# The first MoE of a fused attention, MoE, MoE kernel in token groups of 256 and 512 instead of 256 and 320 by turns

## The chip, the cores and the metric

One Trainium2 chip (trn2); the kernel runs on one of its cores. The metric is the device time of one launch in microseconds (us), from the profile-independent timing of repeated runs; 917.83 us is the median of three runs of the kernel before (917.74 to 920.07).

## The reference

Inputs are q, k, v of 4 batches, 8 heads, 576 positions, head size 64, a row `s` per head, and the weights of two MoEs.

```python
scores = scale * np.matmul(q, k.transpose(0, 1, 3, 2))
cum = np.cumsum(np.maximum(s, 0.0), axis=-1)
bias = -(cum[:, :, :, None] - cum[:, :, None, :])
scores = np.where(causal, -1e9, scores + np.minimum(bias, 0.0))
attn = np.exp(scores - np.max(scores, axis=-1, keepdims=True))
attn = attn / (np.sum(attn, axis=-1, keepdims=True) + 1e-09)
x = attn @ v                          # as (2304 tokens, 512)
h = np.maximum(np.maximum(x @ w1, x @ w2), x @ w3)   # d_ff 768
x = h @ w_out                         # first MoE
return ((x @ w_a) * (x @ w_b)) @ w2_out              # second MoE, d_ff 1536
```

## The kernel before

Everything is fp32. The matmuls of the MoEs take two-term splits: an operand `x` is kept as `xh` (rounded to fp32r) and `xl = x - xh`, and a product is three matmuls, `wh*xh + wh*xl + wl*xh`.

**Attention.** Heads go in pairs (4 a batch), so there are 32 pairs, numbered 0 to 31. A batch's 576 queries are two steps: `R = 0` takes the first 256 queries (a short step), `R = 1` the other 320 (a long step, against all 576 keys). So there are 8 steps, 0 to 7, of 4 pairs each; even steps are short. In steps 0 to 2 the scores are plain fp32 matmuls (`f_unit0`, `f_unit`, `f_joint`); in steps 3 to 7 they are split ones (`s_unit0`, `s_unit`, `s_joint`), for which `split_qk` writes the next pair's q and k in split form into `KB1`, `KB2`, `QA1`, `QA2` (one buffer each). A pair goes through: scores on PE (tiles `f`, `s`, `fj`, `sj`), `softmax` (L398 row maximum on DVE, L405 exp on ACT, L409 and L410 on DVE, L415 scaling on POOL), transposes of the probabilities on PE (`ft`, `t`, `tj`) with ACT copies to `PF`, the product with v (`f_pv`, tile `fpv`), and `f_x`, which writes `Xh` (ACT) and `Xl` (DVE), the split input of the first MoE. V(i) below is the product with v of pair i, S(i) its scores, T(i) its transposes.

**First MoE.** `moe1_units` makes the 22 units of one group of tokens; a group is one step's 256 or 320 tokens. 18 gate units (`gate(m, g)`, tile `g`, L592) are 12 matmuls each, with 128x128 weights and the group's tokens as moving columns; ACT and DVE take the maximum of three (L598, L601) and split it into `hh`, `hl`. 4 output units (`outp(c)`, tile `o`, L620) are 18 matmuls each; their result `xo` is stored to `x2T` in DRAM. So a group is 216 + 72 = 288 matmuls whatever its width. The 24 weight tiles are loaded and split during steps 0 and 1 (`fetch_w1`, `conv_w`).

**Order.** All pieces are put on one axis, `stream`, whose position counts attention steps: the pieces of step n lie between n and n + 1, the MoE units of step n's tokens between n + 1.1 and n + 2.1 (the first group between 1.7 and 2.1). They are emitted in this order, the attention with a raised priority, and the framework's planner orders each engine's queue: by priority among what it reckons ready, so MoE matmuls fill the gaps that a pair's softmax leaves on PE. Each engine then runs its queue in order and waits on semaphores.

```python
m0 = stp + 1 + (M0 if stp == 0 else M1)
m1 = stp + 2 + M1
for n, (c, fn) in enumerate(units):
    todo.append((stp, n, fn))
    stream.append((m0 + (m1 - m0) * acc / tot + 1e-6, 0, m_next))
```

**Loads.** `load_pair` puts a pair's k, q and v into `kraw` and `qvraw`, two buffers each, on SP's queue; the loads of pair i + 2 are emitted behind V(i). `PF` has two buffers (`pt_tile`). `preset` fills the constant parts of `KB2`, `QA1`, `QA2` on POOL at the start.

**Behind the attention.** What is left of the first MoE at position 8 is run as the list `moe`; pieces that load and split the second MoE's first weights and inputs (`at(n)`: `more_raw`, `x2_load`, `x2_split`, `w2_pieces`) are put between its units. The second MoE (L1086) follows, by a seven-product scheme over 384 and then 256 columns.

Of the kernel before, what the change touches and what calls it, by code (L numbers as in the profile page):

```python
# [29 lines left out]
def kernel(  # L30
# [18 lines left out]
    nc = tc.nc  # L49
# [21 lines left out]
    QW = 2 * N1 + 64  # L71

# [22 lines left out]
    const = ctx.enter_context(tc.tile_pool(name="const", bufs=1, side="left"))  # L95
# [9 lines left out]
    wst = tc.alloc_tile_pool(name="wst", bufs=3, side="left")  # L105
    ap_ = tc.alloc_tile_pool(name="attn", bufs=1, side="right")


    ident = const.tile([P, P], F32, name="ident")
    make_identity(nc, ident)  # L110

    maskJ = const.tile([P, S // 2 + 4 * P], BF16, name="maskJ")
# [24 lines left out]
    def pt_tile(shape, dt, nm):  # L137
        return ap_.tile(shape, dt, tag="PT", bufs=2, name=nm)
# [17 lines left out]
    with tc.high_priority(5000):  # L156
        ones = pt_tile([SR, 2, 4 * N1], F32, "ones")[:, 0, : 2 * S]
        cs = pt_tile([SR, 2, 4 * N1], F32, "cs")
        sraw, cum = cs[:, 0, : 2 * S], cs[:, 1, : 2 * S]
# [16 lines left out]
    def store_tails():  # L176
        chl = [
            mp.tile([SR, KC * N1], F32R, tag=f"X{c}1", bufs=1, name=f"c{c}")
# [19 lines left out]
    KB1 = ap_.tile([P, 2, S], F32R, name="KB1")  # L198
    KB2 = ap_.tile([P, 2, S], F32R, name="KB2")
    QA1 = ap_.tile([P, QW], F32R, name="QA1")  # L200
    QA2 = ap_.tile([P, QW], F32R, name="QA2")
# [5 lines left out]
    def preset():  # L207
        nc.gpsimd.memset(f(QA1[:, N1 : N1 + 64]), 0.0)

# [43 lines left out]
    w1o = []  # L253
# [9 lines left out]
    NPRE = 4  # L263
    for p_, n0, n1 in zip(w1p, (0, 6, 11, 18), (6, 11, 18, NPRE - MF)):
        w1_tiles(p_, w1_keys[n0:n1])

    w1_raw = {}

    def fetch_w1(key):
        if key in w1_t:  # L270
            raw = wst.tile([P, WC, 2], I32, tag="wst", name="wraw")
        else:
            if key == w1_keys[NPRE - MF]:
                wst.release()
                w1o.append(
                    tc.alloc_tile_pool(name="w1o", bufs=1, side="left", reuse_waits="tile")
                )
            w1_tiles(w1o[0], [key])
            raw = w1o[0].tile([P, WC, 2], I32, tag="raw", bufs=1, name="wraw")
# [23 lines left out]
    rows_in = []  # L303

    def load_pair(b, p, R):
# [7 lines left out]
        WK, WQV = 2 * S, 2 * N1 + 5 * P  # L313
        if b == 0 and p >= 2 and R == 0 and plain:
            t = mp.tile([P, MF * N1], F32, tag="hh" if bp == 2 else "hl", bufs=1, name="kqv")
            kt_, qt_ = t[:, : 4 * Q0], t[:, 4 * Q0 :]
        else:
            kt_ = ap_.tile([P, WK], F32, tag="sk", bufs=2, name="kraw")
            qt_ = ap_.tile([P, WQV], F32, tag="sq", bufs=2, name="qvraw")
        kn = kt_[:, : 2 * nk]  # L320
        if plain and R == 0:
            qn, vn = kt_[:, 2 * nk : 4 * nk], qt_[:, : nb * P]
            nc.sync.dma_start(kt_[0:66, : 4 * nk], kq0[bp])
        else:
            qn, vn = qt_[:, : 2 * nq], qt_[:, 2 * nq : 2 * nq + nb * P]
        kn = kn.rearrange("p (h c) -> p h c", h=2)
        qn = qn.rearrange("p (h c) -> p h c", h=2)
        if plain:
# [17 lines left out]
        vn = vn.rearrange("p (b f) -> p b f", f=P)
# [7 lines left out]
    def k_tails(b, p, R):  # L354
        nk = Q0 if R == 0 else S
# [3 lines left out]
    def q_tails(b, p, R):  # L359
        nq = Q0 if R == 0 else N1  # L360
# [4 lines left out]
    def split_qk(b, p, R, kn, qn):  # L365
        nk = Q0 if R == 0 else S
# [53 lines left out]
    def smm(ps, p, h, q0, ksl):  # L420
        qs = slice(h * (N1 + 64) + q0, h * (N1 + 64) + q0 + P)
# [23 lines left out]
    def s_joint(p):  # L445

# [130 lines left out]
    def moe1_units(R, b, X):  # L577
        n = Q0 if R == 0 else N1
        col = b * S + (0 if R == 0 else Q0)
        st = {}  # L580

        def gate(m, g):
# [3 lines left out]
            Xh, Xl = X()  # L586
# [9 lines left out]
            if g == 0:  # L596
                st["h"] = mp.tile([P, N1], F32, tag="mt", bufs=2, name="hf")
# [5 lines left out]
            if g == 2:  # L603
                if m == 0:
                    st["hh"] = mp.tile([P, MF, N1], F32R, tag="hh", bufs=1, name="hh")
                    st["hl"] = mp.tile([P, MF, N1], F32R, tag="hl", bufs=1, name="hl")
# [3 lines left out]
        def outp(c):  # L610
# [13 lines left out]
            xo = mp.tile([P, N1], F32, tag="mt", bufs=2, name="xo")  # L624
# [16 lines left out]
    def fetch(i):  # L641
        if i < len(pairs) and i not in nat_of:
            b, R, p = pairs[i]
            nat_of[i] = load_pair(b, p, R)
# [19 lines left out]
    def do_split(i):  # L664
        if split_pair(i):
            b, R, p = pairs[i]
            q_tails(b, p, R)
# [4 lines left out]
    def attn_pieces(i, X):  # L672
# [867 lines left out]
```

## Time and profile before

| what | value |
| --- | --- |
| median of three runs | 917.83 us |
| the profiled execution's own time | 915.72 us |
| its span, first to last instruction | 913.9 us |
| PE busy | 900.2 us (98%), 6296 matmuls |
| DVE, ACT, POOL busy | 592.2, 378.9, 225.7 us |
| share of the chain that ended last: PE | 90% |
| of this, lines L592 and L620 (first MoE) | 25% and 9% |

The profile's busy time of a matmul runs from its start to the modelled end of its passage, and neighbours overlap: a group's mean (say 315 ns) is a duration and not what one more matmul costs. What it costs is its pitch, the distance of two starts. In the chain of work that ended last, stretches of one kind are merged with their time and count, and time by count is the pitch.

### The profile page before, as it was taken

To read this page: it belongs to the slowest core of one execution; us is meant where nothing else is said; L and a number is where in the kernel's file an instruction comes from. 1 tells how busy PE (TensorE), PEld (TensorE's weight loads), DVE (VectorE), ACT (ScalarE), POOL (GpSimd) and SP (SyncE) were. 2 spreads that over 40 slices of the span, in tenths; PEclk is the share of its full clock that TensorE was granted. 3 is DMA by queue.
4 is the path that set the end of the run, shared out by engine and by line. 5 is a ranking of instruction groups with operands and counts; after the bars stand their busy time and mean duration, and the time that the engine had idled before them with its cause. 6 is when DMAs were issued, how large, how long until landed. Compare 5 with 4: busy or idle time off the path is not lost.

```text
span 913.9 us, 17151 instructions
## 1 busy us (share of the span) xinstructions
PE 900.2 (98%) x6296; PEld 849.0 (93%) x6296; DVE 592.2 (65%) x1407; ACT 378.9 (41%) x879; POOL 225.7 (25%) x328
## 2 busy tenths in 40 slices
PE   7999999999999999999999999999999999999998
PEld 7677899989999989999899999999999998999998
DVE  4798535554465544555369567767675868996874
ACT  4665634555446564465433332322322222423321
POOL 6654302222123221232122102111111212321211
PEclk9999999999999999999999999999999999999999
DMA  5665332313223132221143214444443243254331
GB/s 169 224 202 175 90 87 73 98 42 101 70 85 97 43 91 80 85 85 54 41 149 134 88 53 155 152 150 145 144 159 107 107 146 122 77 165 158 117 116 47
DMA packets 55212, 102.36 MB, mean 112 GB/s; under 512 B 5736, under 2 KB 39432, under 8 KB 55128
## 3 DMA queue, kind: packets, MB, share of 16 engines
q1 hardware_dynamic: 50520, 96.54, 33.4%
q10 hardware_dynamic: 4608, 4.72, 1.6%
q8 instruction: 50, 0.82, 0.4%
q14 instruction: 34, 0.28, 0.1%
HBM read 77.29 MB, written 23.94 MB: 111 GB/s over the span
## 4 chain that ended last, share of the span: by engine, by line
PE 90%; DVE 4%; DMA 3%; issue 1%; SPq 1%; ACT 1%; POOL 0%; DVEq 0%; ACTq 0%; POOLq 0%
PE g L592 25%; PE X L1086 23%; PE Z L1086 11%; PE o L620 9%; PE Y L1086 6%; PE fpv L531 5%; PE t L545 3%; PE f L466 2%; PE s L422 2%; PE s L423 1%; DVE slot L897 1%; PE ft L508 1%; DMA wraw<-in_moe_w_dram 1%; PE tj L558 1%; PE sj L456 1%
## 5 line engine op out<-in xcount | busy, mean ns | idle before, releaser
L592 PE MATMUL g<-Xh,hg 128*128 128x256 f32 (+1 forms) x576 | 174.8, 305 | 0.5 <-ACT xo L625 0.5
L592 PE MATMUL g<-Xl,hg 128*128 128x256 f32 (+1 forms) x576 | 173.4, 301 | 0.0
L592 PE MATMUL g<-Xh,lg 128*128 128x256 f32 (+1 forms) x576 | 173.2, 301 | 0.0
L592 PEld LDWEIGHTS g<-Xh,hg 128*128 128x128 f32 x576 | 108.5, 189 | 4.4 <-issue 1.6
L592 PEld LDWEIGHTS g<-Xl,hg 128*128 128x128 f32 x576 | 108.9, 189 | 2.5 <-issue 1.4
L592 PEld LDWEIGHTS g<-Xh,lg 128*128 128x128 f32 x576 | 108.8, 189 | 1.2 <-issue 0.9
L1086 PE MATMUL X<-xh,wh 128*128 128x384 f32 x288 | 97.5, 339 | 1.5 <-ACT u L1127 0.6
L1086 PE MATMUL X<-xl,wh 128*128 128x384 f32 x288 | 96.9, 336 | 0.0
L1086 PE MATMUL X<-xh,wl 128*128 128x384 f32 x288 | 96.9, 337 | 0.0
L88 POOL TENSOR_SCALAR wh<-wval 128x256 fp32r<-128x256 f32 x84 | 41.5, 503 | 190.5 <-DVE wval L891 141.8
L1086 PE MATMUL X<-woh,slot 128*128 128x256 f32 x432 | 81.1, 281 | 0.5 <-ACT ob L1129 0.5
L415 POOL TENSOR_SCALAR P<-P,rs 128x128 f32<-128x128 f32 (+2 forms) x80 | 50.1, 631 | 91.4 <-DVE rs L410 75.0
L601 DVE TENSOR_TENSOR hf<-g,hf 128x256 f32<-128x256 f32 (+1 forms) x96 | 43.5, 453 | 41.5 <-PE g L592 39.4
L897 DVE TENSOR_TENSOR slot<-hraw,slot 128x768 fp32r<-128x768 f32 x60 | 60.5, 1031 | 14.9 <-POOL slot L88 13.7
L1086 PEld LDWEIGHTS X<-woh,slot 128*128 128x128 f32 x432 | 68.0, 189 | 0.7 <-ACT ob L1129 0.7
L897 DVE TENSOR_TENSOR u<-Z,u 128x384 f32<-128x384 f32 x72 | 39.6, 552 | 44.5 <-ACT u L1129 34.0
L405 ACT ACTIVATE P<-P,nm 128x128 f32<-128x128 f32 (+2 forms) x80 | 46.5, 582 | 32.7 <-DVE nm L398 27.1
L1086 PE MATMUL X<-wol,slot 128*128 128x256 f32 x216 | 60.1, 280 | 0.0
L620 PE MATMUL o<-hh,lo 128*128 128x256 f32 (+1 forms) x192 | 58.0, 306 | 0.0
L620 PE MATMUL o<-hl,ho 128*128 128x256 f32 (+1 forms) x192 | 57.8, 303 | 0.0
L620 PE MATMUL o<-hh,ho 128*128 128x256 f32 (+1 forms) x192 | 57.0, 302 | 0.3 <-ACT xo L625 0.3
L398 DVE CUSTOM_DVE_ANT_0 P<-s,maskJ 128x128 f32<-128x128 f32 (+2 forms) x80 | 40.5, 514 | 25.7 <-PE s L423 16.7
(165 smaller groups left out, 2255.9 us busy)
## 6 DMA issues: line engine op xcount, KB each, us to landing
hT<-u SPq DMA_DIRECT2D x72, 192.0 KB
hraw<-hT SPq DMA_DIRECT2D x36, 384.0 KB
wraw<-in_moe_w_dram SPq DMA_DIRECT2D x18, 512.0 KB
wraw<-in_moe_w_out_dram SPq DMA_DIRECT2D x18, 512.0 KB
qvraw<-in_qv_dram SPq DMA_DIRECT2D x12, 640.0 KB
kraw<-in_kT_dram SPq DMA_DIRECT2D x24, 288.0 KB
wraw<-in_moe_w_a_dram SPq DMA_DIRECT2D x12, 512.0 KB
wraw<-in_moe_w_b_dram SPq DMA_DIRECT2D x12, 512.0 KB
```

Source lines behind the costliest of these rows:

```text
L88: nc.gpsimd.tensor_scalar(o, i, scale, 1.0, op0=ALU.mult, op1=ALU.mult)
L398: nc.vector.tensor_tensor_reduce(pt[:, c0 : c0 + w], v_, m_, -scale, first, op0=ALU.add, op1=ALU.min, accum_out=nm[:, i : i + 1],)
L405: e_ = nc.scalar.activation(pt[:, c0:c1], pt[:, c0:c1], AF.Exp, bias=first, scale=-1.0, accum_out=sm[:, g : g + 1],)
L415: nc.gpsimd.tensor_scalar(pt[:, c0:c1], pt[:, c0:c1], rs[:, g : g + 1], 1.0, op0=ALU.mult, op1=ALU.mult,)
L422: nc.tensor.matmul(ps, QA1[:, qs], KB1[:, h, ksl], start=True, stop=False)
L531: nc.tensor.matmul(ps[h * D : h * D + D, c0:n], w, x, start=(t == 0), stop=(t == len(mm[h]) - 1),)
L545: nc.tensor.transpose(ps[:, j * P : j * P + P], pt[:, j * P : j * P + P], ident)
L592: nc.tensor.matmul(ps[:, :n], w[:, kk, :], x[:, kk, :], start=(i == 0), stop=(i == len(mm) - 1),)
L601: st["V"] = nc.vector.tensor_tensor(hf, ps[:, :n], hf, op=ALU.max)
L620: nc.tensor.matmul(ps[:, :n], w[:, c, :], x[:, m, :n], start=(i == 0), stop=(i == len(mm) - 1),)
L897: return {"V": nc.vector, "P": nc.gpsimd}[e].tensor_tensor(o, a, b, op=op)
L1086: nc.tensor.matmul(ps[:, :n], w, x, start=(first and i == 0), stop=(i == len(mm) - 1), skip_group_check=not first,)
```

## The change

The first MoE runs over groups of its own, `GR`: tokens 0 to 256, and then four times 512 (256 to 768, to 1280, to 1792, to 2304). `f_x` cuts a pair's columns where they cross a group's border. The gate and output units get positions of their own (`G0` to `G1` the gates, `G1` to `G2` the outputs). `X` of even groups lies in pool `xA`, of odd ones in `xB`, which earlier hold the weights' raw tiles and the cumulative sums' temporaries. To make room, `PF` of long steps and odd short pairs has one buffer and that of even short pairs another, smaller one; `kraw` and the q part have one buffer (plain even pairs have their own in a pool `px`), v has two; `KB1` to `QA2` take `px`'s place, so `preset` runs only when the first split pair comes (pair 12). The raw weight tile and the `xt` tile of the second MoE share one buffer, and the pieces between the last units lie at other units.

```diff
+    NG = 512
+    GR = [(0, Q0)] + [(c, c + NG) for c in range(Q0, NT, NG)]
...
-    def pt_tile(shape, dt, nm):
-        return ap_.tile(shape, dt, tag="PT", bufs=2, name=nm)
+    def pt_tile(R, p):
+        if R == 0 and p % 2 == 0:
+            return ap_.tile([P, 2, 3 * P], F32, tag="PT0", bufs=1, name="PF")
+        return ap_.tile([P, 2, 4 * N1], F32, tag="PT", bufs=1, name="PF")
...
     def preset():
+        px.release()
+        kqp.append(
+            tc.alloc_tile_pool(name="kb", bufs=1, side="right", reuse_waits="tile")
+        )
+        for nm, w in (("KB1", 2 * S), ("KB2", 2 * S), ("QA1", QW), ("QA2", QW)):
+            t = kqp[0].tile([P, w], F32R, name=nm)
...
+            if b == 1 and p == 3 and R == 0:
+                kt_ = px.tile([P, 4 * Q0], F32, name="kraw3")
+            else:
+                own = plain and p % 2 == 0
+                kt_ = (px if own else ap_).tile([P, 2 * S], F32, tag="sk", bufs=1, name="kraw")
+            vt_ = ap_.tile([P, 5 * P], F32, tag="sv", bufs=2, name="vraw")
...
-    def f_x(R, p, ps, Xh, Xl):
-        n = Q0 if R == 0 else N1
-        rnd("A", Xh[:, p, :], ps[:, :n])
-        sub("V", Xl[:, p, :], ps[:, :n], f(Xh[:, p, :]))
+    def f_x(b, R, p, ps):
+        c0 = b * S + (Q0 if R else 0)
+        c1 = c0 + (N1 if R else Q0)
+        for g, (g0, g1) in enumerate(GR):
+            a, e = max(c0, g0), min(c1, g1)
+            if a < e:
+                Xh, Xl = x_tiles(g)
+                o = slice(a - g0, e - g0)
+                v_ = ps[:, a - c0 : e - c0]
+                rnd("A", Xh[:, p, o], v_)
+                sub("V", Xl[:, p, o], v_, f(Xh[:, p, o]))
...
     def do_split(i):
         if split_pair(i):
             b, R, p = pairs[i]
+            if not kqp:
+                preset()
...
+    G0, G1, G2 = (1.7, 3.02, 5.02, 7.02, 8.0), (2.05, 3.95, 5.95, 7.95, 9.0), (3.0, 5.0, 7.0, 9.0, 9.9)
+    for grp in range(len(GR)):
+        units = moe1_units(grp)
+        k = 3 * MF
         for n, (c, fn) in enumerate(units):
-            todo.append((stp, n, fn))
-            stream.append((m0 + (m1 - m0) * acc / tot + 1e-6, 0, m_next))
-            acc += c
+            todo.append((grp, n, fn))
+            if n < k:
+                at_ = G0[grp] + (G1[grp] - G0[grp]) * n / k
+            else:
+                at_ = G1[grp] + (G2[grp] - G1[grp]) * (n - k) / (len(units) - k)
+            stream.append((at_ + 1e-6, 0, m_next))
...
     stream.append((0.1, 0, tails))
-    stream.append((0.5, 0, preset))
...
-    at(1)(lambda: x2_split(0, 0, 1, q0[0], EN, (0,)))
+    at(3)(lambda: x2_split(0, 0, 1, q0[0], EN, (0,)))
...
+    at(10)(lambda: x2_split(0, 1, 2, q0[0], EN, (0,)))
```

## Rows read from the trace of the kernel before

**Rows 1.** The page, 40 slices: PE's busy tenths and the granted TensorE clock.

```profile
PE   7999999999999999999999999999999999999998
...
PEclk9999999999999999999999999999999999999999
```

**Rows 2.** Chain that ended last, whole span: start, us, engine, tile, line, count.

```profile
194.70 4.07 PE g L592 x34
...
462.77 30.04 PE g L592 x203
```

**Rows 3.** The same chain from 225 to 275 us: a score of 512 columns.

```profile
269.73 0.23 PE s L422
```

**Rows 4.** PE and its weight loads by form: busy us, mean ns, idle before.

```profile
L592 PEld LDWEIGHTS g<-Xl,hg 128*128 128x128 f32 x576 | 108.9, 189 | 2.5 <-issue 1.4 <-DVE Xl L92 0.4
```

**Rows 5.** A stretch of step 2, L592 alone: PE busy (count), PEld busy (count), PEclk, DMA, GB/s.

```profile
113.00:150.00 37.00, 32.22 (x186) 28.13 (x187) 1.00 0.31 81
```

**Rows 6.** The stretch before it, L620 alone, same columns.

```profile
92.00:113.00 21.00, 10.71 (x69) 8.91 (x69) 1.00 0.31 91
```

**Rows 7.** PE in order of time, end of step 1 and step 2: start, us.

```profile
109.39 2.42 PE L531 MATMUL fpv<-PF,qvraw 128*64 128x320 f32 x20
111.74 0.87 PE L508 MATMUL ft<-ident,F 128*128 128x128 f32 x6
...
115.99 0.87 PE L531 MATMUL fpv<-PF,qvraw 128*64 128x256 f32 x8
...
120.00 0.38 PE L466 MATMUL f<-kraw 66*128 66x128 f32 x2
...
120.37 0.59 PE L466 MATMUL f<-kraw 66*128 66x256 f32 x2
...
121.26 0.87 PE L531 MATMUL fpv<-PF,qvraw 128*64 128x256 f32 x8
```

**Rows 8.** The same view, the last product with v of step 2.

```profile
148.74 0.87 PE L531 MATMUL fpv<-PF,qvraw 128*64 128x256 f32 x8
```

**Rows 9.** DVE, ACT and POOL by form from 100 to 450 us.

```profile
L398 DVE CUSTOM_DVE_ANT_0 P<-s,maskJ 128x256 f32<-128x256 f32 x16 | 6.6, 414 | 0.0
...
L398 DVE CUSTOM_DVE_ANT_0 P<-s,maskJ 128x128 f32<-128x128 f32 x16 | 4.6, 286 | 6.7 <-PE s L423 5.8 <-PE g L592 0.8
L405 ACT ACTIVATION_READ_ACCUMULATOR P<-P,nm 128x1 f32 x80 | 15.1, 189 | 0.0
...
L511 ACT COPY PF<-ft 128x384 f32<-128x384 f32 x24 | 11.1, 473 | 10.0 <-PE ft L508 9.7
...
L405 ACT ACTIVATE P<-P,nm 128x256 f32<-128x256 f32 x16 | 8.0, 501 | 0.7 <-DVE nm L398 0.7
...
L405 ACT ACTIVATE P<-P,nm 128x128 f32<-128x128 f32 x16 | 6.3, 397 | 1.7 <-DVE nm L398 0.8 <-DVE rs L410 0.6
L81 ACT ACTIVATE QA<-qvraw 128x512 fp32r<-128x512 f32 x8 | 5.0, 631 | 14.2 <-DMA qvraw<-in_qv_dram 14.2
...
L415 POOL TENSOR_SCALAR P<-P,rs 128x256 f32<-128x256 f32 x16 | 8.3, 516 | 0.0
```

**Rows 10.** All engines in order of time: a load's issue, and its reader.

```profile
222.03 5.30 SPq L343 DMA_DIRECT2D qvraw<-in_qv_dram  x2
...
225.17 0.63 ACT L81 ACTIVATE QA<-qvraw 128x512 fp32r<-128x512 f32 x1 [1.28 <-DMA qvraw<-in_qv_dram]
```

**Rows 11.** POOL in order of time: the longest fill of `preset`.

```profile
1.99 1.05 POOL L210 MEMSET KB<- 64x1152 f32 x1
```

**Rows 12.** PE in order of time: a product with v, the next pair's transposes.

```profile
203.83 2.42 PE L531 MATMUL fpv<-PF,qvraw 128*64 128x320 f32 x20
...
207.11 0.27 PE L558 MATMUL tj<-ident,PJ 128*128 128x128 f32 x1
```

**Rows 13.** Stretches near the start, columns PE, PEld, DVE, ACT, POOL, PEclk, DMA, GB/s.

```profile
12.00:14.00 2.00, 0.00 (x0) 0.00 (x0) 1.40 (x8) 1.75 (x7) 1.44 (x4) 1.00 0.14 37
...
16.00:20.00 4.00, 4.00 (x21) 3.86 (x20) 1.69 (x8) 0.70 (x1) 0.82 (x2) 0.57 0.94 309
```

More of the change, by code (lines that the diff above doesn't have):

```diff
@@ L71 @@
     QW = 2 * N1 + 64
+    NG = 512
+    GR = [(0, Q0)] + [(c, c + NG) for c in range(Q0, NT, NG)]
+    assert GR[-1][1] == NT and len(GR) == 5
     DLY0, DLY1, DLY2, DLY3 = 900, 400, 1500, 1000
@@ L195, in store_tails @@
             nc.sync.dma_start(dq[:, 1, 64:], b[:, 1, :256])
[L198 to L201, printed above, removed]
+    kqp = []
     def heads(t, r0, r1, n):
@@ L207, in preset @@
     def preset():
+        px.release()
[4 more added lines that the diff above has]
+            t = kqp[0].tile([P, w], F32R, name=nm)
+            kqp.append(t.rearrange("p (h c) -> p h c", h=2) if w == 2 * S else t)
+        _, KB1, KB2, QA1, QA2 = kqp
         nc.gpsimd.memset(f(QA1[:, N1 : N1 + 64]), 0.0)
@@ L261, in w1_tiles @@
             w1_t[key] = [pool.tile([P, WC], F32R, name=c + nm) for c in "hl"]
-    NPRE = 4
-    for p_, n0, n1 in zip(w1p, (0, 6, 11, 18), (6, 11, 18, NPRE - MF)):
+    for p_, n0, n1 in zip(w1p, (0, 6, 11, 18), (6, 11, 18, 24)):
         w1_tiles(p_, w1_keys[n0:n1])
     w1_raw = {}
+    wr2 = xA.tile([P, 2, 2 * WC], I32, tag="b", bufs=1, name="wraw")
+    wr1 = wst.tile([P, 2 * WC], I32, name="wraw")
+    wraws = [t.rearrange("p (c t) -> p c t", t=2) for t in (wr2[:, 0], wr2[:, 1], wr1)]
     def fetch_w1(key):
[L270 to L279, printed above, removed]
+        raw = wraws[w1_keys.index(key) % 3]
         if key[0] == "g":
@@ L354, in k_tails @@
     def k_tails(b, p, R):
+        _, KB1, KB2, QA1, QA2 = kqp
         nk = Q0 if R == 0 else S
@@ L359, in q_tails @@
     def q_tails(b, p, R):
+        _, KB1, KB2, QA1, QA2 = kqp
         nq = Q0 if R == 0 else N1
@@ L365, in split_qk @@
     def split_qk(b, p, R, kn, qn):
+        _, KB1, KB2, QA1, QA2 = kqp
         nk = Q0 if R == 0 else S
@@ L420, in smm @@
     def smm(ps, p, h, q0, ksl):
+        _, KB1, KB2, QA1, QA2 = kqp
         qs = slice(h * (N1 + 64) + q0, h * (N1 + 64) + q0 + P)
@@ L445, in s_joint @@
     def s_joint(p):
+        _, KB1, KB2, QA1, QA2 = kqp
         HS = S // 2
@@ L643, in fetch @@
             b, R, p = pairs[i]
-            nat_of[i] = load_pair(b, p, R)
+            if i < NP:
+                nat_of[i] = load_pair(b, p, R)
+            else:
+                with tc.issue_after(last_in[-1] if i > NP else rows_in[NP - 1]):
+                    nat_of[i] = load_pair(b, p, R)
     def split_pair(i):
@@ L764 @@
                 fetch(i)
-        fetch_w1(w1_keys[2])
+        with tc.issue_after(rows_in[2]):
+            fetch_w1(w1_keys[2])
     stream = []
@@ L770, with x_tiles @@
     xt = {}
-    def x_tiles(stp):
-        if stp not in xt:
-            while todo and todo[0][0] <= stp - 2 and todo[0][1] < 3 * MF:
+    def x_tiles(g):
+        if g not in xt:
+            while any(t[0] <= g - 2 and t[1] < 3 * MF for t in todo):
                 todo.pop(0)[2]()
-            R = stp % 2
-            n = N1 if R else Q0
-            xt[stp] = [
-                mp.tile([P, KC, n], F32R, tag=f"X{c}{R}", bufs=1, name=f"X{c}")
-                for c in "hl"
-            ]
-        return xt[stp]
+            n = GR[g][1] - GR[g][0]
+            if g == 0:
+                t = xA.tile([P, 2, KC, n], F32R, tag="a", bufs=1, name="X")
+                xt[g] = [t[:, 0], t[:, 1]]
+            elif g % 2 == 0:
+                if g == 2:
+                    while w1_pend:
+                        load_w1(w1_pend.pop(0))
+                    wst.release()
+                xt[g] = [
+                    xA.tile([P, KC, n], F32R, tag=t, bufs=1, name=f"X{c}")
+                    for t, c in zip("ab", "hl")
+                ]
+            else:
+                xt[g] = [
+                    xB.tile([P, KC, n], F32R, tag=f"X{c}", bufs=1, name=f"X{c}")
+                    for c in "hl"
+                ]
+        return xt[g]
     def m_next():
@@ L836 @@
             fn()
+    assert not any(t[0] < len(GR) - 1 and t[1] < 3 * MF for t in todo)
     moe = [(1, m_next) for _ in range(len(todo))]
+    kqp[0].release()
     ap_.release()
+    xB.release()
     TB = 384
@@ L870, in load_raw @@
         nraw[0] += 1
-        raw = pool.tile([P, WC, 2], I32, tag="raw", bufs=1, name="wraw")
+        if pool is rA2:
+            t = pool.tile([P, 4 * TB], I32, tag="xt", bufs=1, name="wraw")
+            raw = t[:, : 2 * WC].rearrange("p (c t) -> p c t", t=2)
+        else:
+            raw = pool.tile([P, WC, 2], I32, tag="raw", bufs=1, name="wraw")
         rv = raw.rearrange("p c t -> p (c t)")
```

101 lines of the change are left out of this document (49 added, 52 removed).

## The prediction

> **What bounds the kernel now.** I read the slices of the page first. PE is busy in nearly every slice and its granted clock is at the upper level, 2.4 GHz, almost throughout [rows 1]. The reader is to see that no stage behind the first 20 us has a hole that a faster DVE, ACT or DMA would close. The chain of waits says the same: 90% of it is PE, and 34% is the first MoE (table above). So what matters is how long PE takes for a matmul, and whether it always has one to do. For the first I use the chain in order of time, where a run of one kind gives the pitch. For the second I use the stretch tables and PE's order of time around steps 1 and 2, because there the attention has the least MoE work beside it.
>
> **Part 1, wider groups.** Each group costs 288 matmuls whatever its width. Before there are 8 groups, 1152 matmuls of 256 columns and 1152 of 320; after there are one of 256 and four of 512, so 288 and 1152. 864 matmuls go; the columns stay the same.
> Pitches: 34 gate matmuls of 256 columns in 4.07 us are 0.120 us each, 203 of 320 columns in 30.04 us are 0.148 us [rows 2]. At 2.4 GHz the columns alone are 0.107 and 0.133 us, so 13 to 15 ns are fixed in each. Before: 1152 x (0.120 + 0.148) = 308.7 us.
> There is no gate of 512 columns in the trace, but there are fp32r scores of 512. The one shown takes 0.23 us [rows 3]; over seven couples of such scores (48 in all), by the distance of their starts, I read 0.2315. The columns are 0.213 us, so the fixed part would be 18 ns. With the fixed part of the narrower gates it would be 0.228. I take 0.230, nearest to the measured row, and keep 0.228 and 0.2315 as the bounds.
> After: 288 x 0.120 + 1152 x 0.230 = 34.6 + 265.0 = 299.6 us. Gain 9.1 us (7.4 to 11.4). It lies on PE, hence on the path.
>
> **Part 2, where the MoE work lies: step 2.** A wide group can begin only when all its tokens are through the attention. Group 0 is unchanged and is done early: 69 of its 72 output matmuls run between 92 and 113 us [rows 6]. In the 37 us that follow, the next group supplies 186 gate matmuls [rows 5], 186 x 0.148 = 27.5 us, and leaves about 9.5 us to the attention of step 2, whose last product, V(11), comes at 148.7 [rows 8]. Afterwards nothing of this exists: the next group (256 to 768) needs all four pairs of step 2. PE then has only the attention of pairs 8 to 11 until V(11) and its split are done.
> How long is that? The chain of one plain pair, from its first score: 0.95 scores of one head [rows 7], and from [rows 9] 0.70 maxima, 2 x 1.28 for the exps of two heads (each 0.397 + 0.189 + 0.501 + 0.189), 2 x 0.516 scalings, 0.47 copy. With about 0.3 for the small DVE ones, 0.3 for three transposes and 0.87 for V [rows 7] that is 7.2 us. ACT alone needs 2 x 1.28 + 2 x 0.47 + some 0.4 = 3.9 us a pair, so that is the floor of the pace. T(8) is at 111.7 us and V(8) at 116.0 [rows 7], with gates between; without them V(8) follows its copies at about 113.3, and V(9) at 116. S(10) can start when T(8) gives its buffers free, 112.4, so V(10) ends near 119.6 and V(11), a floor later, near 123.5; with the split 124.3. Between 113.6 and 124.3 PE has 9.2 us of scores, transposes and products (3.4 us for each of two whole pairs, 2.4 us for what is left of two). Hole: 1.5 us.
> `preset` moves into this place. Its fills, some of them over 1 us [rows 11], are then on POOL behind S(11), ahead of or between the scalings of pair 11; V(11) waits for those, and pair 12's splits and small SP loads queue behind the fills. I price it at up to 2 us. Pair 12's own wait is hidden by 216 gates, 49.7 us; without these it would be about 4 us of fills and a load. I take 3 us for the hole (1 to 12). The upper end is pairs one by one, 7.2 us each from V(9) at 117 on, so V(11) at 131.4, 9.4 us of hole, and a fall of the clock. The latter exists here: after PE was empty from 12 to 14 us, the granted clock of 16 to 20 us was 0.57, mostly the lower level, 1.2 GHz [rows 13], worth some 1.7 us.
>
> **Part 3, steps 4 and 6.** Gates now lie in long steps, outputs in short ones. A short step has 72 x 0.230 = 16.6 us of outputs and about 2.5 us a pair of attention, 26.5 us, or 6.6 us a pair, where it had some 11. ACT's floor for a split pair is 3.9 + 2 x 0.63 = 5.2 us [rows 9]. One k and q buffer makes a loop: split of pair i + 1, then the load of i + 2, then its split. The split is about 2 us on ACT and DVE; a load was read 3.1 us after its issue [rows 10], so 5 to 6 us with the other issues on SP. Both floors lie just under 6.6. Beyond that PE waits. A pair fully in series, 7.2 + 2, would cost 4 x 2.6 = 10.4 us a step. I take 0.75 us a step, 1.5 in all (0 to 21). The long steps have 49.7 us of gates and are safe.
>
> **Part 4, what I cost at nothing.** One `PF`: already before, the next pair's first transposes in a long step come behind V, which ends at 206.2, at 207.1 [rows 12], so the copy into `PF` meets a free buffer; if it did not, each long pair would wait 2.4 us. Loads of i + 2: on SP their q and k now wait for the split of i + 1, which lies ahead of V(i), and only v waits for V(i), so they come no later; without that lead a load's 3.1 us would lie between pairs. The columns cut at a border add one more ACT and one more DVE instruction to 12 pairs, about 0.3 us each behind V, where PE has other work. The shared raw and `xt` buffer and the moved pieces lie beside 26 units, 4 x 18 x 0.230 + 66.2 = 82.8 us of pure PE work, where 52 us held them before. The second MoE is untouched.
>
> **Sum.** -9.1 + 3 + 1.5 = -4.6 us. Against the profiled execution's own 915.72 that is 911.1 (its span 913.9 to about 909.3); that execution is 2.1 us under the median of the runs, 917.83, and on the median's scale the forecast is 913.2.
>
> **Rivals.**
> *A, even.* The gain is paid back: pairs of steps 4 and 6 at 7.4 us instead of 6.6 cost 6.4 us, the hole 3. Time 918.1. For it: floors of 5 to 6 us stand so near 6.6. Against it: the planner has the attention lead the MoE, so at the end of a long step some gates are left over.
> *B, slower.* The same place, short steps 4 and 6, decides: with a pace of 8 us a pair they cost 4 x 1.4 x 2 = 11.2 us, step 2 stays at 3, together 14.2 against 9.1. Time 922.9. The point from which it decides is a pace of about 7.4 us, where loss and gain meet. For it speaks the full chain of 7.2 us, which overlaps only if scores of the next pair are ready early, and they need the single buffers of `QA1` and k; against it that scores do run ahead: S(10) starts at 120.0 us, V(9) at 121.3 [rows 7].
> *C, a better pitch.* A weight load takes 189 ns [rows 4], longer than a matmul of 256 or 320 columns and shorter than 512. If the fixed part is what is left of that load, it goes: 1152 x (0.230 - 0.213) = 19.6 us more, time 893.6. Against it stands 0.23 [rows 3], fixed part and all. The Trainium skill, "TensorE: Matmul & The Clock Gate", section "Wait — 56ns, not 53.3ns?", states a warm pitch of 215.7 ns at 512 columns, a fixed cost of about 2.5 ns. By it the gain would be 16.5 us larger. Trace and page differ on the narrower gates already, and the measured row decides.
> *D, it does not do what it says.* The gates of 512 columns run at 0.235 or more and the planner pulls them apart by attention pieces: 1152 x 0.235 + 34.6 = 305.3, a gain of 3.4 us, eaten by the hole. Time about 918.9.
>
> **Chances and range.** Forecast 0.50, A 0.20, B 0.20, C 0.04, D 0.06. The forecast's own range, with pitch, hole and short steps at their nearer bounds, is 906 to 916. 0.3% is 2.75 us, about what a measurement of this kernel can tell from no change, so the lines are 915.1 and 920.6. Faster: nearly all of the forecast and C, 0.51. Within: A, D and the forecast's upper tail, 0.28. Slower: B, 0.21. The range must hold 8 in 10: it leaves out C and half of B, 905 to 924.
>
> **What would show it.** Right: L592 and L620 rows of 512 columns, whose runs in the chain give 0.228 to 0.2315 us; PE with few matmuls for 10 us around 115 to 124 us, then gates without a break; steps 4 and 6 with an interval of 6 to 7 us between products with v; a second MoE of the same length. Wrong: a pitch of 0.235 or of 0.216; gaps of PE on `ft` or `s` in short steps that wait for POOL, ACT or a load; a clock under 1.00 in the slices of step 2; ACT copies to `PF` that wait for `fpv`.

## The result: slower by 0.8%

The changed kernel takes 926.67 us (median of four runs, 925.01 to 927.39), the kernel before beside it 918.69: ratio 1.0083, 95% interval 1.0062 to 1.0104. The forecast was 913.2 us, with a range of 905 to 924 us. The two profiled executions differ by more than the medians, 925.6 against 913.9 us of span, because that of before is one of its shortest and that of after its longest. A term of 1 or 2 us that rests on one trace is therefore within what two executions of one kernel can differ.

**The page of after**, its header, PE's busy time, and the slices that answer to [rows 1]:

```profile
span 925.6 us, 15336 instructions
...
PE 906.0 (98%) x5432; PEld 794.6 (86%) x5432; DVE 587.2 (63%) x1365; ACT 376.1 (41%) x843; POOL 222.3 (24%) x328
...
PE   7999979999999999999999999999999999999998
...
PEclk8999999999999999999999999999999999999999
```

864 matmuls are gone, as forecast, and PE is as busy as before. Only one slice behind the start has lost its 9: the sixth, 116 to 139 us, which is step 2.

**Wide gates in the chain of work that ended last** (start, us, line, count), in answer to [rows 2]:

```profile
446.48 48.51 PE g L615 x214
497.93 9.78 PE o L643 x42
```

48.51 / 214 is a pitch of 0.2267 us, a little below the lower bound of the forecast (0.228). The fixed part beyond 512 columns at 2.4 GHz is 0.0134 us, the same 13 to 15 ns that the narrow gates have. The outputs' run, 9.78 / 42, is at 0.233 us, a little over the upper bound (0.2315).

**Step 2 of after, stretches of 5 us**: PE, PEld, DVE, ACT and POOL busy (count), granted clock, DMA share, GB/s.

```profile
126.00:131.00 5.00, 4.53 (x24) 3.66 (x24) 2.64 (x17) 2.29 (x10) 1.65 (x4) 1.00 0.30 87
131.00:136.00 5.00, 0.94 (x8) 0.62 (x6) 2.31 (x9) 3.25 (x8) 4.33 (x7) 0.86 0.50 147
136.00:141.00 5.00, 4.90 (x19) 3.56 (x20) 2.56 (x5) 2.19 (x9) 3.23 (x5) 0.50 0.14 26
141.00:146.00 5.00, 5.00 (x29) 3.86 (x28) 2.15 (x9) 2.07 (x5) 0.75 (x1) 0.95 0.88 244
```

PE is empty for 4 us, and the clock then falls to its lower level, 1.2 GHz, for some 7 us (what 0.86, 0.50 and 0.95 lack in three stretches of 5 us). **PE in order of time there**, in answer to [rows 7, 8]; in brackets what it waited for:

```profile
116.06 2.42 PE L548 MATMUL fpv<-PF,vraw 128*64 128x320 f32 x20
...
121.12 0.87 PE L548 MATMUL fpv<-PF,vraw 128*64 128x256 f32 x8
...
124.82 0.87 PE L548 MATMUL fpv<-PF,vraw 128*64 128x256 f32 x8
125.62 1.58 PE L483 MATMUL f<-kraw 66*128 66x128 f32 x8
...
136.10 0.58 PE L473 MATMUL sj<-KB,QA 128*128 128x288 f32 x1 [4.16 <-ACT KB L84]
...
137.33 1.55 PE L548 MATMUL fpv<-PF,vraw 128*64 128x256 f32 x8
```

V(7) comes at 116.1 us, 6.7 later than before. S(10) starts at 125.6, where before it started at 120.0 [rows 7]. The joint scores of pair 12 (`sj`) stand in PE's queue ahead of V(10) and wait 4.16 us for a split. V(11) is at 143.5.

**The chain in that stretch** says what the split waited for:

```profile
118.53 0.34 SPq L350
...
118.96 3.29 DMA kraw<-in_kq_dram
...
122.28 0.55 SPq L348
...
122.88 0.54 SPq L349
...
123.52 0.35 SPq L350
...
123.91 3.37 DMA kraw<-in_kq_dram
...
129.99 3.69 DMA kraw<-in_kT_dram
...
134.84 1.17 ACT KB L84
...
136.10 0.58 PE sj L473
```

A loop of loads on SP: k and q of pair 10 behind a load of v (L350), k and q of pair 11 behind the next one, then pair 12's. The first of these loads, v of pair 9, waits for V(7), 116.1 to 118.5 us. The second, v of pair 10, waits for no product: V(8) ended at 122.0. It stands behind the row copies of pair 10 (L348, L349), which start at 122.28, when that pair's k and q have landed. So each further pair comes about 5 us behind the one before it. **SP's own order** shows how that differs from before. First before, then after (L323 and L333 are k and q, L338 and L350 v):

```profile
84.47 0.31 SPq L323 DMA_DIRECT2D kraw<-in_kq_dram  x1
...
99.90 0.32 SPq L323 DMA_DIRECT2D kraw<-in_kq_dram  x1
104.26 0.31 SPq L323 DMA_DIRECT2D kraw<-in_kq_dram  x1
109.15 0.36 SPq L323 DMA_DIRECT2D kraw<-in_kq_dram  x1
113.88 8.62 SPq L338 DMA_DIRECT2D qvraw<-in_qv_dram  x3
```

```profile
89.13 0.37 SPq L333 DMA_DIRECT2D kraw<-in_kq_dram  x1
105.53 0.34 SPq L350 DMA_DIRECT2D vraw<-in_qv_dram  x1
107.20 0.32 SPq L333 DMA_DIRECT2D kraw<-in_kq_dram  x1
118.53 0.34 SPq L350 DMA_DIRECT2D vraw<-in_qv_dram  x1
118.96 0.32 SPq L333 DMA_DIRECT2D kraw<-in_kq_dram  x1
123.52 0.35 SPq L350 DMA_DIRECT2D vraw<-in_qv_dram  x1
123.91 0.38 SPq L333 DMA_DIRECT2D kraw<-in_kq_dram  x1
```

Before, k and q of pairs 8 to 11 are all issued by 109.2 us and the v of the later ones after them. After, each load of k and q follows a load of v, and pair 11's is issued at 123.9. The lines that do this belong to the change, but the cut diff ahead does not print them:

```diff
     def fetch(i):
         if i < len(pairs) and i not in nat_of:
             b, R, p = pairs[i]
-            nat_of[i] = load_pair(b, p, R)
+            if i < NP:
+                nat_of[i] = load_pair(b, p, R)
+            else:
+                with tc.issue_after(last_in[-1] if i > NP else rows_in[NP - 1]):
+                    nat_of[i] = load_pair(b, p, R)
```

`last_in[-1]` is the v load of the pair before. In SP's queue, which runs in order, k and q of pair i + 1 so stand behind v of pair i, and that one waits until V(i - 2) has given back one of the two v buffers, as v of pair 9 does here.

### Where the time lies

For a ledger I take three instants, V(7), V(11) and the second MoE's first product. From each I subtract the first MoE's matmuls started by then, at their pitch in a run (0.120, 0.148, 0.2267 us). What is left is attention plus every loss, so narrow and wide groups can be compared. At V(11), for instance, before has 288 matmuls of 256 columns and 185 of 320, 61.9 of 148.7 us, and after 288 and 27 of 512, 40.7 of 143.5. The columns are what is left up to V(7), from there to V(11), and from there to the second MoE's start.

| kernel | to V(7) | to V(11) | to MoE 2 | MoE 2 starts | MoE 2 to its last product |
| --- | --- | --- | --- | --- | --- |
| before | 75.8 | 11.0 | 108.4 | 503.9 | 406.5 |
| after | 83.4 | 19.4 | 114.2 | 512.7 | 409.4 |
| loads free (e1) | 79.0 | 15.4 | 114.1 | 504.3 | 408.4 |
| loads free, `sj` late (e3) | 77.5 | 13.0 | 116.0 | 502.2 | 409.3 |
| old groups, after's loads (e4) | 84.2 | 11.5 | 108.5 | 512.9 | 431.9 |
| old groups, loads free (e6) | 77.9 | 11.5 | 109.4 | 507.7 | 429.4 |
| before, after's loads (e5) | 80.1 | 11.1 | 110.4 | 510.4 | 406.4 |
| before, one `PF` (e8) | 77.0 | 11.7 | 108.4 | 505.7 | 406.3 |
| before, mask moved (e9) | 75.5 | 11.0 | 108.4 | 503.7 | 408.5 |

From before to after: the first MoE's own work falls by 13 us, what is left grows by 7.6, 8.4 and 5.8, and the second MoE by 2.9. Together that is the 11.7 us between the two spans.

Part of the first column is not the kernel's. The granted clock from 10 to 25 us is 0.89 in the traces of before, e3, e5, e6 and e9 and 0.77 in those of after, e1, e4 and e8; 0.12 x 15 us is up to 1.8 us of PE's work, an estimate. So e1 and after can be compared there, and e5 and before, but e1 with before, or e8 with before, only to within that.

### The profile page after: what moved, and what is told of

It reads as the page before. It is cut to its first block, busy times and chain, and to the rows that moved or that the text cites. A ratio compares the mean times of both kernels' runs of the same rounds, so it can differ in the third digit from the quotient of the medians.

```text
span 925.6 us, 15336 instructions
## 1 busy us (share of the span) xinstructions
PE 906.0 (98%) x5432; PEld 794.6 (86%) x5432; DVE 587.2 (63%) x1365; ACT 376.1 (41%) x843; POOL 222.3 (24%) x328
## 4 chain that ended last, share of the span: by engine, by line
PE 90%; DMA 4%; DVE 3%; issue 1%; SPq 1%; ACT 1%; POOL 0%; DVEq 0%; ACTq 0%
PE g L615 24%; PE X L1142 22%; PE Z L1142 11%; PE o L643 8%; PE fpv L548 6%; PE Y L1142 6%; PE t L569 3%; PE f L483 2%; PE s L438 2%; PE s L439 1%; PE ft L525 1%; DMA kraw<-in_kq_dram 1%; DVE slot L946 1%; PE tj L582 1%; PE spin L160 1%
## 5 line engine op out<-in xcount | busy, mean ns | idle before, releaser
L615 PE MATMUL g<-Xl,hg 128*128 128x512 f32 x288 | 113.1, 394 | 0.0
L615 PE MATMUL g<-Xh,lg 128*128 128x512 f32 x288 | 111.9, 393 | 0.0
L615 PE MATMUL g<-Xh,hg 128*128 128x512 f32 x288 | 111.7, 398 | 0.0
L615 PEld LDWEIGHTS g<-Xh,lg 128*128 128x128 f32 x288 | 54.1, 188 | 10.2
L615 PEld LDWEIGHTS g<-Xh,hg 128*128 128x128 f32 x288 | 54.3, 190 | 9.9
L615 PEld LDWEIGHTS g<-Xl,hg 128*128 128x128 f32 x288 | 54.1, 188 | 10.0
L624 DVE TENSOR_TENSOR hf<-g,hf 128x512 f32<-128x512 f32 (+1 forms) x60 | 38.0, 634 | 37.9 <-PE g L615 32.8
L548 PE MATMUL fpv<-PF,vraw 128*64 128x320 f32 (+4 forms) x432 | 58.6, 373 | 0.0
L1142 PEld LDWEIGHTS X<-xh,wh 128*128 128x128 f32 x288 | 54.1, 188 | 3.4 <-ACT s L1179 1.1
L91 POOL TENSOR_SCALAR slot<-hraw 128x768 fp32r<-128x768 f32 x25 | 29.9, 1197 | 106.4 <-PE Z L1142 35.1
```

The costliest lines, as they stand in the source:

```text
L91: nc.gpsimd.tensor_scalar(o, i, scale, 1.0, op0=ALU.mult, op1=ALU.mult)
L548: nc.tensor.matmul(ps[h * D : h * D + D, c0:n], w, x, start=(t == 0), stop=(t == len(mm[h]) - 1),)
L615: nc.tensor.matmul(ps[:, :n], w[:, kk, :], x[:, kk, :], start=(i == 0), stop=(i == len(mm) - 1),)
L624: st["V"] = nc.vector.tensor_tensor(hf, ps[:, :n], hf, op=ALU.max)
L1142: nc.tensor.matmul(ps[:, :n], w, x, start=(first and i == 0), stop=(i == len(mm) - 1), skip_group_check=not first,)
```

## The experiments

Theory L: the order of the loads costs the time. Rival S: the scores of pair 12 that stand ahead of V(10) on PE do. Further rivals: the wide groups themselves, the smaller buffers, the place in memory.

### Loads free, scores late, both (e1, e2, e3)

e1 is after with `fetch` as before:

```diff
-            if i < NP:
-                nat_of[i] = load_pair(b, p, R)
-            else:
-                with tc.issue_after(last_in[-1] if i > NP else rows_in[NP - 1]):
-                    nat_of[i] = load_pair(b, p, R)
+            nat_of[i] = load_pair(b, p, R)
```

> The changed kernel (926.7 us) with one thing undone: a pair's loads are no longer ordered behind the load of v of the pair before on SP's queue. Theory L (late loads: in steps 1 and 2 k of the next pair stands on SP behind a load of v that waits for the product with v of two pairs earlier, so with no MoE work beside it the attention of step 2 runs at the pace of the loads): V(7) comes some us earlier than 116.1, V(11) comes at 130 to 135 instead of 143.5, time 916 to 920. Rival S (the scores of pair 12 stand on PE ahead of V(10) and wait for preset and splits): the wait of 4 to 5 us on PE stays, time 924 to 927. Rival F (nothing but the missing MoE work in step 2): V(11) at 140 or later, time 925 to 927.

Measured: 918.84 us, ratio to before 1.0001 (0.9981 to 1.0020). By the ratios, each within some 2 us, this one edit takes back the whole loss. By the medians, after is 7.98 us over the kernel before beside it and e1 1.34, so 6.6 us; the two kernels' own medians lie 7.8 apart. In the table it is 4.4 us before V(7) and 4.0 in step 2. PE in order of time in step 2 now:

```profile
125.02 0.37 PE L473 MATMUL sj<-KB,QA 128*128 128x288 f32 x1 [0.32 <-ACT KB L84]
...
132.99 0.37 PE L473 MATMUL sj<-KB,QA 128*128 128x288 f32 x1 [1.63 <-DMA QA<-qt]
...
135.08 0.87 PE L548 MATMUL fpv<-PF,vraw 128*64 128x256 f32 x8
```

The wait of 4.16 us is one of 0.32, and another of 1.63 us is left in front of V(11).

The 4.4 us before V(7) are for the greater part something else. From 20 us to V(7) PE is never idle in after. What differs is PE's order at V(5). **V(5) in order of time**, first after, then e1:

```profile
81.34 0.75 PE L548 MATMUL fpv<-PF,vraw 128*64 128x320 f32 x2
82.02 0.33 PE L582 MATMUL tj<-ident,FJ 128*128 128x128 f32 x1
82.28 0.75 PE L548 MATMUL fpv<-PF,vraw 128*64 128x320 f32 x2
```

```profile
84.66 2.16 PE L548 MATMUL fpv<-PF,vraw 128*64 128x320 f32 x16
86.75 0.66 PE L582 MATMUL tj<-ident,FJ 128*128 128x128 f32 x4
```

In after four transposes `tj` stand one by one between couples of V(5)'s 20 matmuls, and the whole product, with two scores and four more transposes inside, lasts 7.30 us. In e1 the `tj` stand in one block, and the product with them and two scores lasts 3.58. Less 0.6 for the four further transposes that is some 3 us. So the edit of the loads also changes the order in which the planner puts PE's work, and that, not a wait for a load, is most of the loss before V(7). Why the planner does so isn't shown.

e2 is after with the joint scores of pair 12 ordered behind V(11):

```diff
+                if i == 12:
+                    with tc.issue_after(pv_done[11]):
+                        st["J"] = s_joint(p)
```

> The changed kernel with one edit: the joint scores of pair 12 are ordered on PE behind V(11). Rival S: the wait of 4.6 us ahead of V(10) goes, V(11) comes 5 to 6 us earlier, the clock stays at the upper level there, time 919 to 921. Theory L: the loads of pairs 10 and 11 land as late as before, V(11) comes at most 3 us earlier, time 923 to 926.

Measured: 928.6 us, ratio 1.0121 (1.0102 to 1.0140). It gains nothing and lies above both ranges; V(11) comes at 141.4, 2.1 us earlier than in after. PE in order of time:

```profile
134.93 1.55 PE L550 MATMUL fpv<-PF,vraw 128*64 128x256 f32 x8 [4.30 <-ACT PF L528]
```

Now V(10) itself waits 4.30 us, for a copy to `PF` that stands on ACT behind pair 12's split (`KB`, L84), and that split waits for the same late load, k of pair 12. So S as a cause of its own falls: it was one of several places where the late load shows.

e3 has both edits.

> Both edits together. If L and S are separate costs, the gains of the two add: 911 to 916, faster than the kernel before. If they are one cost (PE waits for whichever is last), no better than the better of the two: 916 to 920.

Measured: 917.53 us, ratio 1.0003 (0.9993 to 1.0014), 1.3 us under e1 by the medians; the two ratios don't tell them apart. With the load early the order on PE is worth about a microsecond at most.

### What the order costs elsewhere, and what it hangs on (e5, e7)

e5 is the kernel before with the same `issue_after`, v last among a pair's loads.

> The kernel before with one part of the change alone: from pair 5 on the loads of a pair are issued in order, each behind the load of v (here q and v together) of the pair before. Buffers, groups of columns and all else as before. Theory L (the order of the loads costs the time, whatever the groups are): SP's queue is held by each v buffer, k and q of pairs 8 to 11 come some 5 to 15 us later, the early part of the second MoE's start moves from 504 to 510 to 512 us, and the whole takes 924 to 927 us. Rival N (the order costs only where the narrow work of the second group isn't there to fill step 2): the waits appear in SP's queue but TensorE has MoE products for them, 917 to 920 us.

Measured: 919.67 us, ratio 1.0033 (1.0020 to 1.0046), so 2.2 us by the medians and 3.0 by the ratio, at the upper end of N's range. The table says why: 4.3 us before V(7) are there again, but step 2 costs 11.1, as before, since the second narrow group's gates fill it. The 4.3 us come in another way than in after: ten waits of PE of 0.3 to 1.2 us between 31 and 90 us. (Its profiled execution is the slowest of its five, so the 6.5 us at the second MoE's start are too many.) This kernel has the buffers of before, so it doesn't tell the width alone. Narrow groups with after's buffers, e4 and e6 below, start the second MoE 5.2 us apart (512.9 and 507.7), all of it before V(7), where e4 has V(5) broken up as after has (7.30 us against 3.59), and up to 1.8 us of it by the clock at the start; in step 2 both cost 11.5. So what the narrow groups' gates cover is the part in step 2, 4.0 us with wide groups.

e7 is after with the order kept, but on the last load of k and q instead of v:

```diff
-            last_in.append(nc.sync.dma_start(vn, qv[b, p][:, 2 * nq :]).ins)
+            last_in.append(rows_in[-1])
+            nc.sync.dma_start(vn, qv[b, p][:, 2 * nq :])
...
-                nc.sync.dma_start(kn[r : r + 64], kT[b, p, :, :, 0:nk])
-            last_in.append(nc.sync.dma_start(vn, qv[b, p][:, 2 * nq :]).ins)
+                kd = nc.sync.dma_start(kn[r : r + 64], kT[b, p, :, :, 0:nk])
+            last_in.append(kd.ins)
+            nc.sync.dma_start(vn, qv[b, p][:, 2 * nq :])
```

> The changed kernel with the order of the loads kept, but hung on the last load of k and q of the pair before in place of its load of v. Theory L' (it is not an order as such that costs the time, but that k and q of pair i+1 stand behind v of pair i, which waits until the product with v of pair i-2 has given its buffer back): 918 to 920.5 us, as with free loads (918.8), and joint scores of pair 12 without the wait of several us. Rival O (any order between the pairs' loads costs it, since the planner then issues them later): 924 to 927 us.

Measured: 919.87 us, ratio 1.0022 (1.0013 to 1.0032), as L' expected. SP now issues k and q of the last three plain pairs early:

```profile
102.07 0.32 SPq L333 DMA_DIRECT2D kraw<-in_kq_dram  x1
106.55 0.31 SPq L333 DMA_DIRECT2D kraw<-in_kq_dram  x1
110.78 0.42 SPq L333 DMA_DIRECT2D kraw<-in_kq_dram  x1
```

V(5) takes 4.18 us there. So it is not an order as such that costs the time, but an order that puts a load that nothing holds up behind one that waits for a buffer, both by that wait and by the place of V(5) in PE's queue.

### What the width is worth (e4, e6)

e4 is after with the eight groups of 256 and 320 columns at their old positions:

```diff
-    GR = [(0, Q0)] + [(c, c + NG) for c in range(Q0, NT, NG)]
+    GR = [(b * S + r * Q0, b * S + (S if r else Q0)) for b in range(B) for r in (0, 1)]
...
+        m0 = grp + 1 + (M0 if grp == 0 else M1)
+        m1 = grp + 2 + M1
```

> The changed kernel's buffers, load order and late preset with the token groups and positions of the kernel before (eight groups of 256 and 320). Theory L: the late loads are there but 27 us of MoE work in step 2 cover them, so 1 to 4 us over the kernel before, 919 to 923. If buffers and loads cost in every step: 930 or more. If they cost nothing by themselves and only the wide groups lose: within 1 us of the kernel before, 918 to 919.

Measured: 948.32 us, ratio 1.0328 (1.0308 to 1.0348), in the range of "930 or more", but by one place and not by a cost in every step. e6 has the loads free as well, and the pieces at the second MoE's entry at their old units (the text on record means the same eight groups of 256 and 320 columns):

> The changed kernel with the loads free (no order between them) and with the groups of columns of before (256 and 512 in turn, eight... six of them, at their old places in the steps), the pieces at the second MoE's entry moved back to the units at which they stood before; buffers as in the changed kernel. Against the kernel with free loads and wide groups, which starts the second MoE at 504.3 us and takes 918.8, it tells what the width is worth. Theory W (the width gains 7 to 8 us, and the hole of step 2 takes the rest of it back even with free loads): with narrow work to fill step 2 the second MoE starts at 505 to 507 us, 918 to 922 us in all. Rival W0 (the width gains its 7 to 8 us net, and the smaller buffers cost as much somewhere else): start at 511 to 512 us, 925 to 927 us.

Measured: 942.92 us, ratio 1.0292 (1.0275 to 1.0310). No expectation had this total. Both lose over 20 us at the second MoE's entry (last column of the table). PE in order of time in e6:

```profile
517.33 0.69 PE L1137 MATMUL Z<-xh,wh 128*128 128x384 f32 x1 [8.46 <-POOL wh L90]
```

The raw weight and `xt` share one buffer, so their loads and splits run one after the other, and the units of a narrow group don't last long enough to cover that; after has no such wait on PE there. That wait is not the whole loss: the granted clock of e6 is 0.50 from 515 to 535 us, where after has 1.00. **A stretch behind the wait** in e6 (columns as in step 2 above):

```profile
520.00:540.00 20.00, 17.47 (x56) 13.55 (x57) 13.99 (x31) 4.18 (x8) 5.24 (x10) 0.61 0.48 170
```

56 matmuls lie there, and 116 in the same stretch of after. As totals e4 and e6 thus measure the shared buffer with the fall of the clock, and only their start of the second MoE speaks of the width. There e1 stands 3.4 us ahead of e6 (504.3 against 507.7), nearer to W than to W0; 1.1 us of e6's start is one wait for a split (`hl`) on DVE, and e1 had more of the lower clock in its first 25 us. The first MoE's own work is 13 us less in e1, but step 2 costs 15.4 instead of 11.5, and steps 3 to 7 cost 114.1 instead of 109.4. **Gates in step 2, from V(7) to V(11)**, first e6, then e1 (PE busy and count, PEld, clock, DMA, GB/s):

```profile
113.20:152.50 39.30, 32.29 (x188) 28.18 (x187) 1.00 0.24 62
```

```profile
113.60:135.10 21.50, 7.44 (x27) 4.79 (x27) 1.00 0.42 112
```

188 gates there, 27 here: that is the work that used to lie in step 2's gaps.

### One buffer, a pool moved (e8, e9)

e8 is before with `pt_tile` as after has it, and a tile of its own for a temporary (`ones`) that had used it.

> The kernel before with one part alone: a single buffer for the transposed probabilities of the long steps (and one small one, used by every other pair of the short steps), as in the changed kernel, in place of two. Theory (the single buffer costs nothing, as the prediction had it): 917 to 919 us, V(7) at 109 to 110 us. Rival P (the transposes of a pair must wait for the product with v of the pair before, and the single buffer is where the changed kernel loses some 4 us before V(7) even with free loads): V(7) at 112 to 114 us, 920 to 923 us.

Measured: 917.00 us, ratio 0.9997 (0.9987 to 1.0006). One `PF` costs nothing. Rival P had V(7) right (114.2 us in this trace) and the consequence wrong: by then more MoE work was done, and the table has 77.0 against 75.8, no more than the clock of the first 25 us differs.

e9 is before with the identity and the mask in attention's pool, where after has them.

```diff
-    const = ctx.enter_context(tc.tile_pool(name="const", bufs=1, side="left"))
...
-    ident = const.tile([P, P], F32, name="ident")
+    ident = ap_.tile([P, P], F32, name="ident")
...
-    maskJ = const.tile([P, S // 2 + 4 * P], BF16, name="maskJ")
+    maskJ = ap_.tile([P, S // 2 + 4 * P], BF16, name="maskJ")
```

> The kernel before with one part alone: the identity and the mask move from a pool of their own, which lies below everything else, into attention's pool; 2.25 KB per partition less lie below the second MoE's buffers. Theory: nothing, 917 to 919 us, the second MoE takes 410 us from its first product to the end of its last. Rival M (the second MoE takes 2 to 3 us longer in the changed kernel because its buffers lie over others than before and so wait for other readers): the second MoE takes 412 to 413 us, 920 to 921 us in all.

Measured: 919.60 us, ratio 1.0023 (1.0011 to 1.0035): 2.1 us, and the second MoE takes 408.5 us in place of 406.5, the 2 us that rival M expected. But M's reason, a wait for other readers, isn't what the rows show. **PE by form, second MoE's last part** (busy us, mean ns of one, idle before), first before, then e9:

```profile
L1086 PE MATMUL X<-woh,slot 128*128 128x256 f32 x432 | 81.1, 281 | 0.5 <-ACT ob L1129 0.5
...
L1086 PE MATMUL Y<-woh,slot 128*128 128x256 f32 x120 | 23.2, 280 | 0.4 <-DVE s L897 0.4
```

```profile
L1085 PE MATMUL X<-woh,slot 128*128 128x256 f32 x432 | 82.0, 282 | 0.5 <-ACT ob L1128 0.5
...
L1085 PE MATMUL Y<-woh,slot 128*128 128x256 f32 x120 | 23.6, 282 | 0.4 <-DVE s L896 0.4
```

The waits are the same, and the same matmuls take a little longer, up to 2 ns each.

### Later gates, the mask back (e10, e11, e12)

e10 is e3 with the first group's gates as late as they can stand:

```diff
-    G0, G1, G2 = (1.7, 3.02, 5.02, 7.02, 8.0), (2.05, 3.95, 5.95, 7.95, 9.0), (3.0, 5.0, 7.0, 9.0, 9.9)
+    G0, G1, G2 = (1.85, 3.02, 5.02, 7.02, 8.0), (2.17, 3.95, 5.95, 7.95, 9.0), (3.0, 5.0, 7.0, 9.0, 9.9)
```

> The kernel with free loads and late joint scores of pair 12 (917.5 us), and the gates of the first group, of 256 columns, spread over steps 1.85 to 2.17 in place of 1.70 to 2.05: as late as they can stand, since the X of the third group lies where that of the first lay, so that the first pair of step 2 can write its result only when these gates are done. Theory F (step 2 is short of MoE work, and what is moved into it fills gaps there without opening others in step 1): V(11) 2 to 4 us later than 131.2 with as much more MoE work done, the second MoE's start 1 to 3 us earlier than 502.2, 914.5 to 916.5 us. Rival G (step 1 then has the gaps): 917 to 920 us.

Measured: 919.44 us, ratio 1.0015 (0.9993 to 1.0037): no gain, as G expected. V(7) comes 1.5 us later than in e3's trace (in e12 0.4 later than in e11), and no gate more lies in step 2.

e11 is e3 with the mask back in a pool below everything:

```diff
+    const = ctx.enter_context(tc.tile_pool(name="const", bufs=1, side="left"))
...
-    maskJ = ap_.tile([P, S // 2 + 4 * P], BF16, name="maskJ")
+    maskJ = const.tile([P, S // 2 + 4 * P], BF16, name="maskJ")
```

> The kernel with free loads and late joint scores of pair 12 (917.5 us), and the mask back in a pool of its own below everything else (1.6 of the 2.1 KB that stood there before; the identity finds no room). Theory A (the second MoE's products are 0.5 to 1% slower where its buffers lie lower, as in the kernel before with the mask and identity moved away: 408.5 against 406.5 us): the second MoE takes 406.5 to 408 us, 915 to 916.5 us in all. Rival: the 0.5 KB that lack decide, or it is no matter of places: 409 us for the second MoE, 917 to 918 us.

Measured: 916.52 us, ratio 0.9985 (0.9971 to 0.9999), the second MoE 407.2 us in place of 409.3. The same form as above stands at its old duration again:

```profile
L1149 PE MATMUL X<-woh,slot 128*128 128x256 f32 x432 | 81.2, 281 | 0.5 <-ACT ob L1192 0.5
```

It is the fastest kernel of the study: 1.1 us under the before beside it, with an interval that just excludes 1, where after is 8.0 over its own.

> Both edits of the two kernels before this one together. If each gains and they add up: 912.5 to 915 us, faster than the kernel before (917.5 us) and than the changed one. If neither does: 917 to 919 us.

e12, both edits: 917.91 us, ratio 1.0005 (0.9995 to 1.0014). The edits don't add up. The late gates cost 1.4 us here and 1.9 in e10.

## Why the prediction was wrong

**What bounds the kernel** was right: PE, and whether it has work.

**Part 1.** The mechanism was right and the size came near through two errors. The pitch in a run of gates is 0.2267, not 0.230, so the first MoE's own gain is 308.7 - 34.6 - 261.2 = 12.9 us, not 9.1, and beyond the upper bound of 11.4 (11.2 us, if all outputs go at the 0.233 of their run). Against it, steps 3 to 7 hold some 5 us more than with narrow groups and the same buffers (114.1 in e1, 109.4 in e6), which the sum did not have. Net that is 8 us. It is no wait: PE's idle times from V(11) to the second MoE add up to 2.0 us in e1 and 1.7 in e6. That it comes from the attention's matmuls having fewer narrow ones to run between is a reading that no run isolates. Rival C fell, since the fixed part is that of the narrow gates, and rival D's 0.235 fell for a run. The Trainium skill, "TensorE: Matmul & The Clock Gate", section "Wait — 56ns, not 53.3ns?", has 215.7 ns at 512 columns. The trace's 226.7 ns, for gates that each bring their own weights, differ from it, and the measurement decides.

**Part 2.** The place was right and the size (3 us, 1 to 12) lies in the range: step 2 costs 8.4 us more. The step that failed in it is "S(10) can start when T(8) gives its buffers free, 112.4": it took the loads of pairs 10 and 11 as there. S(10) started at 125.6 because its k and q were issued at 119.0. V(11), reckoned for 123.5, came at 143.5; with free loads it comes at 135.1. 4.0 of the 8.4 us go with free loads, and 3.9 are the missing gates (15.4 in e1, 11.5 in e6). The fall of the clock came, from 1.00 to 0.86, 0.50 and 0.95 in three stretches of 5 us. `preset` wasn't tried alone.

**Part 3 and rival B.** Steps 4 and 6 cost nothing by waiting: PE is busy all of 222 to 252 us. **Two stretches of steps 4 and 6 in after**, columns as above:

```profile
222.00:252.00 30.00, 30.00 (x170) 23.74 (x169) 13.73 (x55) 17.10 (x48) 7.66 (x14) 1.00 0.51 153
328.00:358.00 30.00, 30.00 (x171) 23.89 (x170) 13.08 (x48) 16.08 (x46) 7.68 (x14) 1.00 0.48 145
```

A pair there takes about 8 us, which is B's pace, yet PE has MoE work throughout, so the pace isn't a loss. B's time, 922.9 us, came nearest of all by luck: its place was wrong.

**Part 4 is the step that failed.** "On SP their q and k now wait for the split of i + 1 ..., and only v waits for V(i), so they come no later" looked at each load's own buffer and not at its place in the queue. The change hangs k and q of a pair on the v load of the pair before, so they inherit its wait for a product with v. This was priced at nothing and costs 6.6 to 7.8 us: about half of it is the late load in step 2, and the other half, before V(7), mostly the place of V(5) in PE's queue, which changes with the same edit. The prediction named the price itself, a load's 3.1 us between pairs "without that lead", and put no chance on it. "The second MoE is untouched" failed as well: moving the mask and identity shifts its buffers, 2.1 us. One `PF` and the moved pieces were right, the latter because wide units cover them, as e6 shows from the other side.

**The sum.** By the medians: 8.0 us slower, 6.6 to 7.8 of it the order of the loads and 2.1 the moved pool (1.0 us of that came back in e11 with most of the pool). That leaves a gain of some 1 to 2 us for all the rest: the width's net gain of 8 less the 3.9 of the missing gates in step 2 and less what the other buffers cost before V(7) (3.2 us in e1's trace, of which the clock at the start has up to 1.8). These are single traces. What makes up the rest before V(7) stays open.

## What to carry to other kernels

When buffers are cut, write down the order of the queue that fills them: a load whose own buffer is free still comes late if it stands behind one that waits, and hanging it on a load without a wait gets most of the time back. Such an edge in one queue can also change the order in which the planner fills another, so compare both queues before a cost is put down to a wait. Wider work units gain per instruction and take away the small work that filled the gaps of a latency-bound stage, so price the stage they leave as well as the one they speed up. A wait at the head of one queue is seldom its own cause: reordering PE alone (e2) only moved the same 4 us to the next instruction, whose copy stood behind the split of that load.

## What the runs showed of the hardware

The same second-MoE matmuls take 280 and 281 ns in before and 281 in e11, and 282 in e9, where buffers lie up to 2.1 KB lower per partition; that is 2.0 us over that MoE. Why the place matters isn't shown. A gap of 4 us on PE was followed by some 7 us at the lower clock (granted clock 0.86, 0.50 and 0.95 in three stretches of 5 us in after), so the gap cost more than its length: 8 matmuls of a product with v that take 0.87 us at 124.82 took 1.55 us at 137.33. Two matmuls of V(5) and one transpose, taking turns, take 0.94 us (81.34 to 82.28 in after); 16 such matmuls and four transposes, each kind in a block, take 2.58 us (84.66 to 87.24 in e1). The fixed part of a matmul with its own weight load stayed at 13 to 15 ns from 256 to 512 columns, although the weight load's 189 ns [rows 4] are longer than the narrow passages and shorter than the wide one.
